# A new order of issue for the first third of a memory-attention and SwiGLU kernel

## The chip, the cores and the metric

The kernel runs on one core of a Trainium2 chip. The metric is the device time of one execution in microseconds, as the median of several runs. The core has five engines that run side by side, each with its own instruction stream: TensorE (PE, its weight loads shown apart as PEld), VectorE (DVE), ScalarE (ACT), GpSimd (POOL) and SyncE (SP), which here only starts DMA transfers.

## The reference

The inputs are q, k and v of 8 batches x 8 heads x 576 positions x 64, phi of 8 x 8 x 576 x 32, and the weights of a gated feed-forward layer, 512 wide with 1536 hidden columns.

```python
a = exp(phi - max(phi, axis=2)); a = a / (sum(a, axis=2) + 1e-9)      # softmax over the 576 positions
k_m = einsum('bhsm,bhsd->bhmd', a, k); v_m = einsum('bhsm,bhsd->bhmd', a, v)   # 32 memory slots
scores = q @ k_m^T / 8
attn = softmax(scores) @ v_m                                          # over the 32 slots
x = attn, heads side by side: 4608 x 512
xn = x / sqrt(mean(x * x) + 1e-6) * rms_g
g = xn @ w_gate; val = xn @ w_val
out = (g * sigmoid(g) * val) @ w_out
```

The three weight matrices arrive as 64-bit floating-point numbers, so they are loaded as pairs of 32-bit words and converted on the chip. q and k are large (factors of 200), and the products of the feed-forward layer are taken with every operand split into a high and a low part, three matmuls for one.

## The kernel before

All work is cut into 2785 small parts, Python functions that each issue a few instructions: one group of matmuls, one copy, one load. The program makes them in one numbered list, and `perform` calls them in the order of the list of numbers `ISSUE`. Nothing else sets the order: the scheduler of the framework is off. Each engine executes its own instructions strictly in the order in which the parts issue them, so one list sets five orders, and an instruction that has to wait holds all that stands behind it on its engine. SP is such an engine too: a load whose buffer is not free holds the loads behind it.

The parts, by stage:

- Softmax of phi (`prep`, lines 362 to 436): PE transposes a maximum (L377) and sends it back (L398), DVE subtracts it from phi (L407), ACT takes the exponential (e_bd, L416), POOL makes the sums (es, L434).
- k_m and v_m (`kv_steps`, lines 440 to 533): matmuls of k and v with e_bd (kvp, L461) and of ones with the sums (L471), scaling, transposes (kvt, L511), and copies by ACT, km (L519, part 57 for batch 0) and vt (L525). k and v of batches 0 and 1 come in large pieces (kvs, `load_half`, L334, parts 37 to 40 for batch 1), those of the others head pair by head pair (`load_kv`, L347).
- Pair 0, that is batches 0 and 1, in its own form: pieces of q (qs, L546, parts 33 to 36 and 41 to 44, two for a block of heads), a copy by ACT that orders a block (qr, L553), transposes by PE (qtp, L567) and copies of the turned q (qT, L573), scores (S, L589), their softmax on DVE and ACT (L594 to L624), x by matmuls (xp, L845), its squares summed by ACT (L856), 1/rms by a Newton iteration on DVE (L866 to L891), diagonal matrices of 1/rms by ACT (first, L803, parts 189, 190, 197), and the product of x with them by PE (ts, L811, part 191 the first, part 205 the first of the second half), whose high part ACT copies (ath, L830) and whose low part DVE makes (atl, L826).
- The later pairs (`attend_steps`): fetches of q (L645; one part is two DMA issues; parts 439 to 442 and 444 to 447 for batch 2), transposes by DVE (L654), scores (S, L670), softmax (L681 to L718).
- Weights: a load of a 128-column block of one of the three matrices (`load_w`, L927 for w_out, L930 for the others; part 810 is the third block of w_out), conversion on ACT, DVE and POOL (wex, mi, L944 to L989) into wc (gate and value) or oh and ol (w_out), a store of the converted block to DRAM (L994, L996), and later a reload (L1013, L1016) whenever a column is wanted again. wc has three buffers; raw, oh and ol two.
- The feed-forward work, in 48 column steps (12 blocks of hidden columns for each of 4 pairs): for a pair and a block of 128 hidden columns, the weights are multiplied by v_m first (vp, L1034, PE; high part xh by ACT, L1051, low part xl by DVE, L1049; parts 1118 and 1120 are the first two such copies). Then come groups of six matmuls for gate and value (pg, pv, L1069; parts 1122, 1123, 1126, 1127 and 1147 are some of the first), the gate function by ACT (L1080), the product by DVE (hf, L1085), its high part by ACT (hh, L1095) and low part by POOL (hl, L1100), and the matmuls with w_out (po, L1126), whose sum ACT or DVE adds up (acc, L1135, L1137).

PSUM, which takes the results of matmuls, is split into four banks that scores and products share and two buffers for vp.

Of the kernel before, what the change touches and what calls it, by code (L numbers as in the profile page):

```python
# [31 lines left out]
    31, 0, 37, 12, 38, 39, 13, 1, 40, 19, 14, 15, 20, 42, 2, 3, 21, 16, 17, 4, 5, 34, 22, 23, 24, 36, 18, 6,  # L32
    45, 46, 47, 25, 7, 41, 8, 9, 10, 11, 48, 43, 33, 35, 752, 745, 49, 26, 44, 60, 61, 27, 236, 52, 50, 28,
    51, 53, 55, 95, 54, 29, 223, 30, 127, 62, 57, 56, 275, 58, 63, 753, 96, 67, 64, 85, 777, 65, 755, 86, 66,
    770, 68, 32, 59, 75, 70, 238, 87, 76, 754, 72, 746, 756, 69, 757, 795, 71, 88, 77, 747, 105, 78, 97, 748,
    749, 98, 89, 79, 90, 750, 91, 237, 115, 80, 239, 106, 224, 107, 118, 81, 73, 116, 119, 128, 130, 131, 82,
    129, 751, 758, 225, 83, 92, 151, 108, 99, 117, 120, 93, 226, 84, 139, 760, 100, 94, 152, 109, 101, 110,
    102, 111, 227, 153, 112, 228, 103, 132, 778, 154, 155, 104, 113, 229, 230, 114, 74, 140, 133, 168, 121,
    134, 779, 135, 122, 231, 163, 141, 142, 169, 123, 232, 143, 164, 156, 233, 771, 136, 144, 124, 125, 165,
    137, 259, 157, 126, 145, 166, 138, 772, 167, 170, 781, 171, 172, 774, 240, 782, 146, 241, 773, 775, 234,  # L40
    158, 159, 1117, 173, 780, 147, 242, 148, 190, 235, 1118, 149, 274, 160, 1120, 197, 243, 150, 1119, 272,
    189, 191, 192, 161, 1121, 162, 174, 273, 260, 776, 175, 179, 783, 176, 796, 244, 245, 180, 798, 246, 797,
    761, 249, 247, 799, 196, 261, 194, 250, 177, 248, 198, 251, 800, 252, 178, 802, 253, 262, 254, 762, 784,
    763, 256, 764, 263, 765, 181, 182, 264, 1142, 193, 827, 766, 265, 199, 759, 183, 255, 801, 200, 266, 195,
    1123, 803, 804, 276, 805, 1122, 767, 806, 807, 1143, 201, 1145, 1144, 267, 268, 257, 820, 1146, 808, 277,
    278, 828, 202, 830, 184, 185, 186, 439, 269, 270, 271, 444, 279, 829, 1126, 831, 832, 187, 188, 785, 1127,
    1124, 440, 821, 1128, 822, 442, 204, 1125, 203, 258, 210, 280, 823, 441, 824, 281, 211, 205, 206, 208,
    212, 445, 825, 826, 833, 1185, 446, 217, 218, 768, 447, 282, 285, 286, 283, 810, 284, 209, 215, 287, 769,
    786, 1129, 289, 207, 213, 216, 288, 290, 214, 221, 222, 219, 291, 220, 787, 1132, 293, 789, 790, 788, 443,
    1130, 845, 791, 1152, 292, 448, 1131, 1136, 1133, 1138, 1134, 1137, 792, 1135, 811, 793, 449, 1139, 1186,  # L50
    1147, 1188, 812, 794, 1148, 814, 1149, 1140, 450, 1151, 815, 451, 1153, 1141, 813, 848, 1158, 1150, 816,
    462, 1154, 1157, 452, 1155, 852, 1162, 453, 1156, 846, 834, 1159, 1161, 454, 455, 847, 1167, 1160, 1210,
    849, 850, 1169, 870, 851, 1168, 465, 456, 853, 1171, 855, 463, 854, 457, 856, 458, 1172, 459, 1163, 1211,
    1173, 857, 871, 1170, 877, 858, 1174, 464, 1187, 1189, 1164, 1194, 460, 1165, 1190, 873, 1195, 461, 1192,
    1213, 872, 1204, 467, 1166, 874, 875, 876, 466, 1179, 835, 1180, 470, 1183, 1196, 1212, 1214, 878, 879,
    468, 881, 880, 1181, 882, 883, 1184, 469, 1191, 838, 836, 1193, 837, 902, 1175, 1197, 1198, 1205, 1199,
    1176, 1177, 1182, 839, 840, 471, 1178, 860, 841, 905, 295, 809, 817, 859, 472, 842, 474, 473, 1200, 475,
    1201, 1202, 476, 477, 861, 1229, 863, 903, 862, 1206, 1216, 818, 478, 294, 819, 864, 1203, 904, 1215,
    1217, 865, 866, 1207, 895, 479, 480, 481, 1225, 1219, 1218, 482, 1220, 1221, 843, 483, 896, 1230, 898,
    1222, 1223, 844, 484, 1226, 1208, 906, 488, 1227, 485, 1231, 1209, 1224, 1237, 489, 897, 899, 486, 900,  # L60
    1235, 920, 907, 487, 490, 901, 1228, 927, 1232, 309, 506, 296, 1233, 503, 507, 1239, 508, 1234, 1241, 504,
    921, 491, 908, 909, 1238, 505, 310, 492, 493, 1240, 1243, 928, 1236, 494, 923, 1245, 922, 930, 495, 924,
    925, 509, 496, 497, 885, 1253, 929, 510, 931, 498, 1251, 499, 932, 500, 910, 501, 502, 1246, 1254, 1256,
    926, 1255, 523, 1257, 1278, 524, 1252, 1321, 525, 1247, 1279, 1242, 526, 527, 945, 1280, 886, 308, 1258,
    884, 1244, 1281, 887, 1262, 1260, 889, 888, 1249, 890, 1248, 891, 892, 949, 1250, 1268, 1259, 1270, 1272,
    1261, 911, 1282, 297, 913, 1269, 298, 933, 912, 1264, 1263, 914, 1273, 1265, 1322, 915, 1297, 1271, 893,
    1274, 1266, 956, 1283, 1299, 1287, 950, 894, 1275, 1323, 1285, 1284, 951, 952, 916, 1294, 934, 1293, 947,
    511, 1267, 1286, 1324, 1325, 299, 1289, 1288, 959, 953, 1346, 1276, 512, 513, 514, 515, 516, 1389, 528,
    1290, 1291, 1298, 517, 518, 519, 520, 867, 521, 868, 522, 535, 1295, 529, 1277, 1292, 1296, 1330, 536,
    1300, 1301, 1327, 530, 1326, 1302, 1336, 1328, 954, 1311, 1338, 1329, 533, 935, 869, 1332, 534, 531, 1347,  # L70
    532, 999, 1348, 539, 1307, 1312, 540, 957, 300, 537, 538, 955, 301, 1315, 1308, 1349, 1350, 302, 1316,
    1340, 1313, 1314, 1331, 1333, 1341, 311, 1334, 303, 1337, 304, 936, 1303, 331, 958, 1339, 960, 1342, 1317,
    1304, 961, 938, 1335, 1343, 1390, 1392, 974, 1344, 1351, 1305, 1353, 312, 1306, 1391, 1393, 1365, 1345,
    313, 1414, 305, 962, 314, 977, 937, 963, 1319, 332, 306, 345, 975, 1367, 307, 344, 1352, 1309, 939, 1318,
    940, 981, 917, 1320, 346, 333, 1354, 1355, 976, 978, 1310, 1362, 1357, 1356, 979, 1361, 941, 1358, 989,
    334, 347, 1366, 335, 336, 942, 1363, 1394, 943, 1359, 1364, 1395, 1415, 1417, 1368, 337, 918, 1404, 1396,
    1369, 919, 982, 1406, 1360, 944, 980, 1371, 1377, 338, 1372, 1397, 990, 1375, 1370, 984, 1416, 992, 1418,
    991, 993, 1405, 315, 348, 316, 339, 1407, 317, 1419, 318, 320, 319, 1376, 1381, 321, 322, 323, 1409, 994,
    1421, 324, 964, 325, 995, 1382, 1398, 326, 983, 1400, 349, 328, 985, 1378, 1457, 986, 350, 1010, 987,
    1408, 541, 340, 327, 1399, 1001, 329, 967, 988, 1458, 1379, 1401, 965, 1459, 1373, 1380, 1013, 966, 341,  # L80
# [1150 lines left out]
```

## Time and profile before

| what | value |
| --- | --- |
| median of three runs | 796.77 us (792.98 to 798.15) |
| the profiled execution's own time | 792.07 us |
| its span | 790.3 us |
| mean granted clock of TensorE | 0.991 |
| PE busy | 748.9 us (95% of the span), 7496 matmuls |
| PEld busy | 639.0 us (81%) |
| DVE busy | 471.8 us (60%) |
| ACT busy | 350.9 us (44%) |
| POOL busy | 244.4 us (31%) |
| DMA | 112.86 MB, mean 143 GB/s |

The profiled execution lies 4.7 us under the median, and its span leaves 1.8 us of its time outside. The busy shares are means over the whole span. In forty equal slices of the span PE's busy share is 4, 7, 7, 7, 9, 8 and 8 tenths in the first seven, and nine tenths or more in all but two of the others; the granted clock is under nine tenths of full speed in the second slice alone. A line of the trace gives start, duration, engine, line and operation, and in brackets the idle time that the engine had before it and what ended that.

### The profile page before, as it was taken

The page shows a single profiled execution, that of the slowest core. Times are in us where ns is not written, and L with a number is a line of the kernel's source. Part 1 is how long each engine was busy: PE and PEld are TensorE (multiplying, and loading weights), DVE is VectorE, ACT ScalarE, POOL GpSimd, SP SyncE. Part 2 cuts the span into 40 slices and gives each one's busy share as a digit, 9 for nine tenths or more (in the row PEclk, how much of TensorE's full clock was granted, in tenths as well). Part 3 has the DMA queues.
Part 4 walks back from the last instruction along what each step waited for, and adds up shares of the span by engine and source line. Part 5 has one row for each costly group of instructions (what it writes and reads, how often), then busy time and mean ns, then how long its engine had stood idle before and what let it go on. Part 6 is the DMA issues. An engine that isn't in the chain of part 4 may idle for free.

```text
span 790.3 us, 18128 instructions
## 1 busy us (share of the span) xinstructions
PE 748.9 (95%) x7496; PEld 639.0 (81%) x7496; DVE 471.8 (60%) x956; ACT 350.9 (44%) x697; POOL 244.4 (31%) x209
## 2 busy tenths in 40 slices
PE   4777988999999999999999999899999999999998
PEld 2565766788887988888888888788888888888886
DVE  6698878888776676465565374655454422444443
ACT  1668767665555544532354334442432335232221
POOL 0244555354432223322433212221232212121212
PEclk9799999999999999999999999999999999999999
DMA  9947775856583652253153654222241334112113
GB/s 331 375 148 214 200 184 198 275 177 213 196 216 85 198 152 95 80 174 98 67 181 123 153 170 99 86 81 71 92 134 54 117 110 147 53 56 80 54 54 120
DMA packets 111722, 112.86 MB, mean 143 GB/s; under 512 B 61460, under 2 KB 77848, under 8 KB 111640
## 3 DMA queue, kind: packets, MB, share of 16 engines
q1 hardware_dynamic: 111640, 111.70, 45.2%
q8 instruction: 59, 0.97, 0.5%
q14 instruction: 23, 0.19, 0.1%
HBM read 89.66 MB, written 22.02 MB: 141 GB/s over the span
## 4 chain that ended last, share of the span: by engine, by line
PE 81%; DVE 6%; ACT 5%; DMA 4%; SPq 2%; issue 1%; POOL 0%; ACTq 0%; DVEq 0%
PE po L1126 36%; PE pg L1069 17%; PE pv L1069 17%; PE vp L1034 5%; PE xp L845 2%; SPq L645 2%; DMA kvs<-in_k_dram 1%; PE kvp L461 1%; DMA qs<-in_q_dram 1%; PE S L670 1%; ACT wex L944 1%; DVE phi L407 1%; ACT xh L1051 1%; DMA raw<-in_moe_w_out_dram 1%; ACT L1080 1%
## 5 line engine op out<-in xcount | busy, mean ns | idle before, releaser
L1100 POOL TENSOR_TENSOR hl<-hf,hh 128x512 fp32r<-128x512 f32 (+1 forms) x84 | 120.0, 1431 | 311.8 <-ACT hh L1095 297.9
L1085 DVE TENSOR_TENSOR hf<-pv,sg 128x256 f32<-128x256 f32 (+1 forms) x192 | 85.5, 452 | 153.1 <-PE pv L1069 110.1
L1126 PE MATMUL po<-oh,hh 128*128 128x512 f32 x432 | 172.2, 399 | 2.3 <-ACT acc L1135 1.4
L1080 ACT ACTIVATE sg<-pg 128x256 f32<-128x256 f32 (+1 forms) x192 | 77.6, 411 | 213.9 <-PE pg L1069 183.3
L1137 DVE TENSOR_TENSOR acc<-po,acc 128x512 f32<-128x512 f32 x180 | 121.0, 685 | 84.5 <-PE po L1126 84.0
L1126 PE MATMUL po<-oh,hl 128*128 128x512 f32 x432 | 170.2, 394 | 0.0
L1126 PE MATMUL po<-ol,hh 128*128 128x512 f32 x432 | 169.2, 392 | 0.0
L1095 ACT CAST hh<-hf 128x512 fp32r<-128x512 f32 (+1 forms) x96 | 64.5, 675 | 86.5 <-DVE hf L1085 86.2
L1126 PEld LDWEIGHTS po<-oh,hh 128*128 128x128 f32 x432 | 81.1, 188 | 21.8 <-ACT acc L1135 2.2
L1126 PEld LDWEIGHTS po<-oh,hl 128*128 128x128 f32 x432 | 81.2, 188 | 17.9
L1126 PEld LDWEIGHTS po<-ol,hh 128*128 128x128 f32 x432 | 81.2, 188 | 13.5
L1069 PE MATMUL pv<-ath,xh 128*128 128x320 f32 (+1 forms) x384 | 84.6, 301 | 4.3 <-ACT sg L1080 3.3
L1069 PE MATMUL pg<-ath,xh 128*128 128x256 f32 (+1 forms) x384 | 85.8, 305 | 2.4 <-DVE hf L1085 1.4
L1069 PE MATMUL pv<-ath,xl 128*128 128x320 f32 (+1 forms) x384 | 81.4, 293 | 0.0
L1069 PE MATMUL pg<-ath,xl 128*128 128x256 f32 (+1 forms) x384 | 81.3, 293 | 0.0
L1069 PE MATMUL pg<-atl,xh 128*128 128x256 f32 (+1 forms) x384 | 81.3, 293 | 0.0
L1069 PE MATMUL pv<-atl,xh 128*128 128x320 f32 (+1 forms) x384 | 81.3, 293 | 0.0
L1049 DVE TENSOR_TENSOR xl<-vp,xh 128x512 fp32r<-128x512 f32 x96 | 64.3, 682 | 28.0 <-ACT xh L1051 27.8
L1069 PEld LDWEIGHTS pg<-ath,xh 128*128 128x128 f32 x384 | 62.7, 188 | 16.7 <-issue 5.0
L1069 PEld LDWEIGHTS pv<-ath,xh 128*128 128x128 f32 x384 | 63.4, 188 | 15.3 <-ACT sg L1080 5.3
L1051 ACT CAST xh<-vp 128x512 fp32r<-128x512 f32 x96 | 54.3, 590 | 29.8 <-PE pv L1069 11.7
L1069 PEld LDWEIGHTS pv<-atl,xh 128*128 128x128 f32 x384 | 61.3, 188 | 0.0
(121 smaller groups left out, 998.0 us busy)
## 6 DMA issues: line engine op xcount, KB each, us to landing
wc<-wd SPq DMA_DIRECT2D x36, 512.0 KB, 5.5
oh<-od SPq DMA_DIRECT2D x36, 256.0 KB, 3.6
ol<-od SPq DMA_DIRECT2D x36, 256.0 KB, 3.9
out_dram<-acc SPq DMA_DIRECT2D x36, 256.0 KB, 2.2
q<-in_q_dram SPq DMA_DIRECT2D x96, 72.0 KB, 2.9
raw<-in_moe_w_val_dram SPq DMA_DIRECT2D x12, 512.0 KB, 4.7
raw<-in_moe_w_gate_dram SPq DMA_DIRECT2D x12, 512.0 KB, 4.5
raw<-in_moe_w_out_dram SPq DMA_DIRECT2D x12, 512.0 KB, 4.7
```

Source lines behind the costliest of these rows:

```text
L645: load(d["q", cc][32 * g:32 * g + 32, s], q[b, 4 * cc + 2 * s + h].rearrange("(r x) d -> r x d", r=32)[:, :, 32 * half:32 * half + 32],)
L845: nc.tensor.matmul(xp[64 * j:64 * j + 64, s, t - t0, P * cc:P * cc + P], st["at", pr][rows, t, cc, 64 * j:64 * j + 64], st["kb", 2 * pr + ...
L1034: nc.tensor.matmul(vp[32 * g:32 * g + 32, flip(b, cc), cc, :], vm[pr][rows, b, hp, 32 * (g % 2):32 * (g % 2) + 32], w[rows, hp, :], start= ...
L1049: V.tensor_tensor(out=xl[:, k], in0=src, in1=xh[:, k].bitcast(F32), op=ALU.subtract)
L1051: nc.scalar.copy(xs[i][0][:, k], src)
L1069: nc.tensor.matmul(pt[:, :N], l[:, flip(b, cc), cc, half * P:half * P + P], r[:, b, cc, t0:t0 + n, :].rearrange("p t x -> p (t x)"), start ...
L1080: nc.scalar.activation(sg[:, :N], acts[gi, b, 0][:, :N], AF.Silu)
L1085: V.tensor_tensor(out=acts[gi][:, :, b, :], in0=acts[gi, b, 1][:, :N].rearrange("p (t x) -> p t x", x=64), in1=acts[gi, b, 2][:, :N].rearr ...
L1095: nc.scalar.copy(hh, acts[gi].rearrange("p t b x -> p t (b x)"))
L1100: (V if gi and i < 12 else nc.gpsimd).tensor_tensor(out=hl, in0=acts[gi].rearrange("p t b x -> p t (b x)"), in1=hsplit[i, gi][0].bitcast(F ...
L1126: nc.tensor.matmul(po, l[:, tt, :], r, start=(m == 0), stop=(m == 5))
L1137: V.tensor_tensor(out=accs[key], in0=pt[0], in1=accs[key], op=ALU.add)
```

## The change

Only the list `ISSUE` changes. Its first 1325 numbers are put in another order, the same 1325 numbers; the last 1460 stand as they were, broken into lines elsewhere. Every part, tile, shape and buffer count stays as it is. In the trace of before the first 1325 parts fill about the first 306 us, and from the 1251st number on the two lists run side by side again but for a few parts (367, 909, 1043 to 1047, 1053) that the new list has later or earlier.

Below, the first lines of the diff and those that hold the parts named here.

```diff
--- before.py
+++ after.py
@@ -29,156 +29,159 @@
 ON_SCALAR = 21
 
 ISSUE = [
-    31, 0, 37, 12, 38, 39, 13, 1, 40, 19, 14, 15, 20, 42, 2, 3, 21, 16, 17, 4, 5, 34, 22, 23, 24, 36, 18, 6,
...
-    158, 159, 1117, 173, 780, 147, 242, 148, 190, 235, 1118, 149, 274, 160, 1120, 197, 243, 150, 1119, 272,
-    189, 191, 192, 161, 1121, 162, 174, 273, 260, 776, 175, 179, 783, 176, 796, 244, 245, 180, 798, 246, 797,
-    761, 249, 247, 799, 196, 261, 194, 250, 177, 248, 198, 251, 800, 252, 178, 802, 253, 262, 254, 762, 784,
...
-    278, 828, 202, 830, 184, 185, 186, 439, 269, 270, 271, 444, 279, 829, 1126, 831, 832, 187, 188, 785, 1127,
-    1124, 440, 821, 1128, 822, 442, 204, 1125, 203, 258, 210, 280, 823, 441, 824, 281, 211, 205, 206, 208,
-    212, 445, 825, 826, 833, 1185, 446, 217, 218, 768, 447, 282, 285, 286, 283, 810, 284, 209, 215, 287, 769,
...
-    1502, 1551, 1038, 1500, 1496, 1053, 1540, 1504, 363, 566, 1542, 1507, 365, 1552, 1505, 1511, 1039, 1040,
-    1506, 1509, 557, 1508, 1041, 1046, 558, 1517, 1044, 1042, 1553, 367, 1512, 1523, 1018, 1518, 567, 1510,
...
+    40, 31, 39, 12, 13, 14, 0, 1, 2, 3, 4, 5, 6, 19, 20, 15, 16, 17, 34, 18, 7, 21, 22, 23, 24, 45, 46, 36,
+    8, 9, 25, 26, 10, 32, 27, 28, 47, 11, 37, 48, 38, 60, 49, 61, 29, 30, 52, 51, 54, 33, 75, 62, 63, 50,
+    53, 67, 35, 85, 42, 76, 77, 64, 66, 86, 55, 56, 87, 65, 68, 70, 69, 71, 57, 752, 753, 754, 756, 43, 72,
...
+    783, 146, 147, 158, 761, 795, 798, 173, 762, 159, 160, 238, 240, 148, 241, 190, 189, 235, 242, 243, 161,
+    244, 1117, 796, 1118, 1120, 191, 197, 192, 194, 797, 162, 149, 245, 799, 150, 274, 1119, 800, 801, 179,
...
+    1144, 195, 269, 270, 1146, 829, 202, 767, 186, 187, 831, 1126, 200, 759, 1122, 1128, 832, 820, 821, 256,
+    784, 188, 822, 1147, 1124, 217, 1123, 1125, 444, 271, 279, 439, 280, 203, 204, 210, 1127, 824, 205, 281,
+    1129, 218, 823, 825, 826, 282, 206, 207, 208, 209, 221, 283, 285, 222, 286, 284, 287, 219, 220, 211,
+    833, 289, 212, 213, 214, 1132, 785, 786, 787, 215, 216, 789, 1130, 442, 1134, 441, 440, 810, 445, 443,
...
+    1597, 1555, 1017, 569, 572, 1559, 1561, 973, 1560, 1034, 1041, 1618, 570, 571, 573, 1514, 1002, 998,
+    1055, 574, 1557, 1538, 1539, 1556, 1558, 1619, 1019, 1042, 1608, 1573, 1620, 1609, 1621, 1574, 575,
+    1610, 1598, 1562, 1000, 909, 1563, 1564, 1622, 1612, 1614, 1053, 1611, 576, 1043, 1600, 577, 380, 1624,
...
```

Some of the moves: of SP's parts, the order 37, 38, 39, 40, then q pieces 42, 34, 36, 41, 43, 33, 35 becomes 40, 39, 34, 36, 37, 38, 33, 35, 42, 43, 41. Of ACT's, 190, 1118, 1120, 197, 189 becomes 190, 189, 796, 1118, 1120, 197. Of PE's, the parts between 186 and 205, which were 279, 1126 and 1127, become 1126, 1122, 1147, 1123, 279, 1127. Of SP's, 439, 444, 440, 442, 441, 445, 446, 447, 810 becomes 444, 439, 442, 441, 440, 810, 445, 446, 447, with 785 among them. The store of column 6 (part 909) goes from the 632nd place to the 1263rd, the reload of column 8 (945) from the 683rd to the 751st, that of column 13 (1001) from the 979th to the 1145th, that of column 16 (1053) from the 1163rd to the 1269th.

## Rows read from the trace of the kernel before

**Rows 1.** Windows by stage: us, each engine's busy time, granted clock, DMA share, GB/s

```profile
0.00:49.00 49.00, 30.09 (x589) 22.15 (x589) 33.66 (x107) 23.31 (x46) 11.05 (x20) 0.90 0.90 319
49.00:74.00 25.00, 18.52 (x509) 15.06 (x510) 22.43 (x59) 19.01 (x47) 12.04 (x16) 0.93 0.57 182
74.00:90.00 16.00, 13.00 (x125) 10.44 (x126) 12.88 (x41) 10.52 (x26) 8.18 (x7) 1.00 0.81 173
90.00:134.00 44.00, 38.27 (x328) 30.13 (x327) 36.83 (x61) 33.59 (x59) 20.81 (x15) 1.00 0.73 207
134.00:200.00 66.00, 65.09 (x733) 54.54 (x734) 56.45 (x111) 39.43 (x81) 31.26 (x28) 1.00 0.67 222
200.00:290.00 90.00, 89.73 (x885) 77.29 (x884) 61.83 (x119) 48.26 (x88) 29.70 (x25) 1.00 0.59 165
290.00:790.30 500.30, 494.22 (x4336) 429.42 (x4334) 247.74 (x462) 176.74 (x357) 131.31 (x102) 1.00 0.32 103
```

**Rows 2.** Three ten-microsecond windows of the start, same columns

```profile
0.00:10.00 10.00, 1.55 (x5) 0.72 (x5) 5.38 (x25) 1.28 (x1) 0.70 (x6) 1.00 0.80 272
20.00:30.00 10.00, 6.46 (x148) 4.28 (x132) 3.02 (x17) 3.97 (x8) 0.09 (x1) 0.60 1.07 378
30.00:40.00 10.00, 8.01 (x110) 6.18 (x108) 9.46 (x23) 8.80 (x20) 4.31 (x5) 0.89 1.08 373
```

**Rows 3.** Timeline of PE: start, duration, instruction, idle before it and releaser

```profile
19.53 0.89 PE L461 MATMUL kvp<-kvs,e_bd 64*32 64x128 f32 x44 [1.42 <-DMA kvs<-in_v_dram]
...
26.92 0.69 PE L511 MATMUL kvt<-ident,vb 128*128 128x128 f32 x2 [2.32 <-ACT km L519]
...
56.34 2.08 PE L811 MATMUL ts<-first 128*128 128x128 f32 x8 [2.68 <-ACT first L803]
...
73.88 0.50 PE L1069 MATMUL pg<-ath,xh 128*128 128x256 f32 x2
...
74.69 0.40 PE L1069 MATMUL pv<-ath,xh 128*128 128x256 f32 x2
...
77.66 2.05 PE L811 MATMUL ts<-first 128*128 128x128 f32 x16 [2.10 <-ACT first L803]
...
286.64 1.09 PE L1034 MATMUL vp<-wc,vm 64*32 64x256 f32 x32
...
294.77 1.96 PE L1034 MATMUL vp<-wc,vm 64*32 64x256 f32 x64
```

**Rows 4.** Chain of waits: start, length, what the end waited on

```profile
17.92 7.93 DMA qs<-in_q_dram
...
25.87 0.72 ACT qr L553
...
54.74 0.96 ACT xh L1051 x2
...
84.70 4.58 DMA raw<-in_moe_w_out_dram
```

**Rows 5.** Timeline of ACT, same columns as PE's

```profile
54.34 0.40 ACT L803 ACTIVATE first<-ident,rinv 128x128 f32<-128x128 f32 x1 [0.86 <-DVE rinv L891]
...
89.30 0.66 ACT L944 ACTIVATE wex<-raw 128x512 f32<-128x512 f32 x1 [2.54 <-DMA raw<-in_moe_w_out_dram]
```

**Rows 6.** Timeline of DVE, same columns

```profile
76.72 0.17 DVE L891 SCALAR_TENSOR_TENSOR rinv<-u,rinv 128x5 f32<-128x5 f32 x1
```

**Rows 7.** Timeline of SP's queue: start, time of the run, instructions

```profile
74.90 9.69 SPq L645 DMA_DIRECT2D q<-in_q_dram  x12
```

**Rows 8.** DMA issues of 0 to 50 us: KB each, us to landing

```profile
qs<-in_q_dram SPq DMA_DIRECT2D x8, 288.0 KB, 10.2
```

**Rows 9.** DMA issues of the whole span, same columns

```profile
raw<-in_moe_w_gate_dram SPq DMA_DIRECT2D x12, 512.0 KB, 4.5
wc<-wd SPq DMA_DIRECT2D x36, 512.0 KB, 5.5
wd<-wc SPq DMA_DIRECT2D x12, 512.0 KB, 6.0
```

282 rows, old and new, of the table ISSUE are left out of this document.

## The prediction

> **What bounds the kernel now.** I read the stages first, then TensorE's (PE's) idle times, then the chain of waits, and last the queues that feed the stages. The stages [rows 1] say where an order of issue can still gain. From 290 us on PE is busy 494.2 of 500.3 us, and the two lists are the same there. Ahead of it PE idles 18.9 us up to 49, 6.5 up to 74, 3.0 up to 90, 5.7 up to 134, then 0.9 and 0.3: 35.3 us, of which 34.1 lie ahead of 134 us. The first ten microseconds hold 8.45 of that [rows 2], spent on the first loads and the first softmax, with which both lists begin. So 25.65 us are open to the change. They are no single wait. DVE is busy 22.4 of 25 us and 36.8 of 44 us in two of these stages [rows 1], so there the second engine is nearly as full as the first; and from 20 to 40 us the DMA share is above 1 while DVE has only 3.0 us of work in the first half [rows 2]: the start waits for data, the rest for conversions and evacuations. What PE waits for is seen at its gaps [rows 3]: 1.42 us for a v piece, 2.32 us for ACT's copy of km, 2.68 us and 2.10 us for the diagonals of 1/rms ("first").
>
> The profiled execution took 792.07 us. The median is 796.77, 4.7 us above it. I work out differences against the profiled execution and add them to the median.
>
> **The change, part by part.** No part is added or taken away, so the engines' work is the same; only waits move.
>
> *The start.* SP's list has two q pieces ahead of the last two k and v pieces of batch 1, and three q pieces fewer ahead of the last piece of each of the first two q blocks. A q piece is 288 KB [rows 8], and the queue moves about 378 GB/s [rows 2], so a piece is 0.78 us: k and v of batch 1 land 1.6 us later, and the q blocks 2.3 us sooner. Before, ACT stood at a q copy until 25.87 with the copy of km queued behind it (chain of waits [rows 4]), and PE idled 2.32 us for that copy [rows 3]. In the new list ACT begins with the q blocks that land early, and the copy of km stands behind two q copies and two copies of turned q. I take the 2.32 us as gone and the 1.6 us as paid at the 1.42 us wait for v: -0.7. The bounds are -2.3 (kvs hidden) and +1.6 (the copy of km as late as before, now behind the four copies).
>
> *The first diagonals.* On ACT the list had one diagonal (part 190), two evacuations of vp (0.96 us in the chain [rows 4]), then the other diagonals; the new list has 190, 189, one conversion, then the evacuations. The first matmul of the turn by 1/rms started at 56.34 after 2.68 us [rows 3], from a first diagonal at 54.34 [rows 5]. The evacuations no longer stand between, so -1.0. DVE's chain that makes 1/rms ends the rest of that wait, and stays. Bounds 0 (the conversion, or a later ACT, takes their place) and -2.7.
>
> *The second diagonals.* In the old list only two groups of gate matmuls and a sum stand between the last matmul that makes x (part 186) and the second turn (part 205). PE runs out at the end of the second group and idles 2.10 us until 77.66 [rows 3], because 1/rms is ready at 76.9 on DVE [rows 6]. The new list puts three more groups there (1122, 1147, 1123). A group of six is 0.81 us (from 73.88 to 74.69 [rows 3]), so 2.4 us fill the 2.1: -2.1. But two of the three ran in the stage before 74 us and one near its old place ahead of 90, where they filled PE while DVE was late; there up to 2.4 us of PE time now stand open. Between 0 and +2.4 I take +2.0, near the upper end since DVE is busy 22.4 of 25 us in that stage [rows 1].
>
> *Third w_out block.* Its load (part 810) stood behind the last twelve fetches of q, which took SP 9.69 us [rows 7], 0.81 each; in the new list three parts of two fetches stand behind it instead of ahead of it, so it is issued 4.8 us sooner. It landed 4.58 us after its turn in the chain of waits [rows 4], and ACT stood 2.54 us for it at 89.30 [rows 5]. That wait goes. The last two q fetches come 0.6 us later, and DVE's transposes of them with it, and the matmuls S behind. PE got only part of ACT's 2.54 us: -1.0, bounds -2.5 and +0.6.
>
> *90 to 134 us.* PE's 5.7 us [rows 1] are many short waits behind evacuations by ACT and DVE. By the lists, of the four PSUM banks that hold scores and products, on average 3.45 are held between the 420th and the 600th part before and 2.39 after: consumers stand closer to producers, and a matmul is less often issued with no free bank. Half of the idle time: -3.0, bounds -5.7 and +2 (DVE is full in 36.8 of 44 us, and a matmul issued sooner may meet a later DVE). The Trainium skill, Perfetto Trace Analysis, section Optimization Strategy, says that the same gap repeating on the engine that should be saturated can mean too little PSUM for the next tile. By that rule the whole 5.7 us would go and the sum would be 2.7 us lower; the trace shows the waits, but not what bank each lacked. From 134 to 290 us only 1.2 us is left [rows 1]; -0.5.
>
> *Late loads.* Some seven conversions now have their load 2 to 5 us of PE's work ahead of them, against 4.5 us of landing [rows 9], and three weight columns (8, 13 and 16) are reloaded closer to their use. The tightest is column 16: its buffer is the one from which column 15 is stored, 6.0 us, and then read, 5.5 us [rows 9]: 11.5 us against 8.1 us from column 15's matmuls at 286.64 to column 16's at 294.77 [rows 3], 3.4 us short if nothing else stands between. These loads start when a buffer is free, which is mostly earlier than their place says: +1.0, bounds 0 and +10.2 (three columns late by 3.4).
>
> **Sum**: -0.7 -1.0 -2.1 +2.0 -1.0 -3.0 -0.5 +1.0 = -5.3: 786.8 against the profiled execution's 792.1, **791.5 us** against the median.
>
> **The rivals.** *The front's idle time mostly goes.* If half of the open 25.65 us goes, the time is 796.8 - 12.8 = 784. For it: the gaps that it names are removed in several places at once, and banks are held shorter. Against it: DVE is nearly full from 30 to 134 us, and its work is the same. The Trainium skill, Perfetto Trace Analysis, section Identifying the Most-Contended Engine, judges PE by the busy share of its weight loads instead of matmuls. As rows: weight loads are busy 209.6 of 290 us, and 429.4 of 500.3 after that [rows 1], 72% against 86%; at 86% the first part would take 244 us, so 46 us would be open and not 35, less the first 8.45; half of it gives 778. The mix of matmuls differs between the two parts, so I give this only 0.05 of the rival's chance of 0.28.
>
> *Nothing is gained, for DVE sets the front.* The list is executed as it stands, so it does what it says on every engine; but where DVE's work from 30 us on is the bound, a gap that is closed on PE opens at the next wait. 797, within 2 us: 0.12.
>
> *Slower: weights come late.* Place: the three reloaded columns and the seven loads. Price: 10.2 us if each column is late by 3.4, plus 0.5 of PE's time for each of seven conversions (the 3.5 us middle of the covers is 1.0 short of 4.5 landing, half of it passed on): 13.7. The start, the first diagonals and w_out still gain 2.7: 796.8 + 11 = 808. It decides from the point at which the matmuls of a column wait over 1 us for a load. For it: shorter covers; against it: PE lacks 1.2 us in all from 134 to 290 us before, so buffers are far ahead there. 0.20.
>
> **How the numbers follow.** My forecast has 0.40 and a range of its own of 786 to 797. A measurement of this kernel can tell about 1% from no change: 788.8 to 804.7. Faster than that is most of the first rival (0.25) and the lower edge of mine (0.09): 0.34. Slower is most of the slower rival, 0.16. Within it is the rest, 0.50. The range 780 to 806 leaves out the lowest of the first rival (0.08) and the upper half of the slower one (0.10).
>
> **What would show it.** Right: no 2.3 us gap of PE for km near 25 us; the turn by 1/rms under 1.7 us of wait, and at its second block none; new PE waits between 60 and 72 us; ACT not waiting for w_out near 89; PE's idle time from 90 to 134 under 3.5 us; from 290 us on the same length as before within 1 us. Wrong: idle time up to 74 us larger by over 3 us, or a wait for a weight column between 150 and 300 us.

## The result, and the profile after

The new list takes 807.21 us (median of 4 runs, 804.05 to 807.58) against 795.62 us: a ratio of 1.0137, 95% interval 1.0093 to 1.0181. It is **slower by 1.4%**, outside the range of 780 to 806 and on the other side of the forecast. The profiled execution took 804.05 us with a span of 802.3 us, 12.0 more than before.

The windows by stage of the new list, in the columns of [rows 1] (line numbers are 3 higher in the new kernel):

```profile
0.00:49.00 49.00, 28.37 (x557) 22.70 (x557) 32.80 (x102) 22.51 (x44) 9.34 (x17) 0.90 0.85 300
49.00:74.00 25.00, 17.05 (x517) 13.14 (x518) 23.58 (x62) 18.75 (x45) 13.35 (x16) 1.00 0.59 202
74.00:90.00 16.00, 12.17 (x96) 10.40 (x95) 12.67 (x42) 11.05 (x27) 7.72 (x9) 1.00 0.84 162
90.00:134.00 44.00, 36.76 (x312) 29.21 (x312) 38.06 (x53) 28.76 (x50) 17.60 (x12) 1.00 0.70 198
134.00:200.00 66.00, 61.88 (x726) 49.91 (x732) 59.54 (x105) 40.64 (x82) 34.04 (x30) 1.00 0.52 172
200.00:290.00 90.00, 88.79 (x868) 76.62 (x869) 64.35 (x122) 46.27 (x86) 31.23 (x26) 1.00 0.57 159
290.00:802.30 512.30, 505.96 (x4436) 439.74 (x4434) 255.19 (x474) 181.89 (x367) 135.47 (x105) 1.00 0.34 110
```

PE's idle time grows in every stage ahead of 290 us: 20.6 us (18.9 before), 8.0 (6.5), 3.8 (3.0), 7.2 (5.7), 4.1 (0.9), 1.2 (0.3). That is 9.7 us in all, of a span that is 12.0 longer; part of the rest is the last 1460 parts, the same in both lists, which took 1.9 us longer in this execution. TensorE's clock is not what was lost: the granted clock up to 74 us is 0.90 and 1.00 of full speed, before it was 0.90 and 0.93 [rows 1], and from there to 290 us it is 1.00 in both. **DVE's busy time** is the other thing to see. It is 486.2 us over the span and was 471.8, with the same 956 instructions. Paired part by part, with the operations' times added up, the first 1325 parts hold all of it: 260.9 us before, 276.0 now. Of these 15.1 us, 5.7 are in the clips and shifts (TENSOR_SCALAR on a weight block), 4.1 in hl, 1.7 in the third step of the conversions (wex<-raw,wex) and 1.6 in the softmax's subtraction (ex<-ex,mx).

PE's timeline of the new list, the waits that answer to [rows 3] and the new ones:

```profile
15.27 0.45 PE L401 MATMUL mr<-ident,mb 128*128 128x128 f32 x1 [2.58 <-DVE mb L396]
...
29.56 1.44 PE L592 MATMUL S<-km,qT 128*64 128x64 f32 x30 [0.49 <-ACT km L522]
...
34.43 1.12 PE L592 MATMUL S<-km,qT 128*64 128x64 f32 x16 [1.74 <-ACT qT L576]
...
51.91 1.02 PE L464 MATMUL kvp<-kv,e_bd 64*32 64x128 f32 x11 [1.53 <-ACT xp L859]
...
58.09 1.16 PE L814 MATMUL ts<-first 128*128 128x128 f32 x8 [0.48 <-ACT first L806]
...
78.93 2.05 PE L814 MATMUL ts<-first 128*128 128x128 f32 x16 [0.84 <-ACT first L806]
82.93 0.71 PE L814 MATMUL ts<-first 128*128 128x128 f32 x4 [1.95 <-ACT first L806]
...
100.59 0.51 PE L1129 MATMUL po<-oh,hl 128*128 128x512 f32 x1 [1.64 <-POOL hl L1103]
...
107.73 0.51 PE L1129 MATMUL po<-oh,hh 128*128 128x512 f32 x1 [2.10 <-DVE hf L1088]
...
121.34 1.17 PE L673 MATMUL S<-qT,km 64*32 64x288 f32 x24 [1.89 <-DVE qT L657]
...
129.48 0.50 PE L1072 MATMUL pv<-ath,xh 128*128 128x256 f32 x2 [1.16 <-DVE hf L1088]
...
148.12 0.51 PE L1129 MATMUL po<-oh,hl 128*128 128x512 f32 x1 [0.87 <-DVE hl L1103]
```

The first k matmuls now follow a transpose at 15.27 us that waited for DVE; before they ran from 12.4. The wait ahead of the first turn by 1/rms is 0.48 instead of 2.68 us, yet the turn starts 1.7 us later, since PE waited ahead of it at other places: the 2.32 us for the copy of km [rows 3] are down to 0.49, but 1.74 us for turned q and 1.53 us for the squares of x have come. The 2.10 us ahead of the second turn are now 0.84, and 1.95 ahead of its last part. From 100 us on stand waits of a length that before had not (its longest from 90 to 150 us is 0.78): for POOL's hl, DVE's hf, DVE's turned q.

What DVE and POOL did ahead of the first two of these is in their timelines. DVE of the new list:

```profile
96.27 1.70 DVE L700 TENSOR_TENSOR ex<-ex,mx 128x1152 f32<-128x1152 f32 x1
97.89 1.51 DVE L951 TENSOR_SCALAR wex<-wex 128x512 f32<-128x512 f32 x1
99.32 1.90 DVE L1103 TENSOR_TENSOR hl<-hf,hh 128x640 fp32r<-128x640 f32 x1
...
105.43 1.84 DVE L963 TENSOR_SCALAR wex<-wex 128x512 int32<-128x512 int32 x1
107.19 0.48 DVE L1088 TENSOR_TENSOR hf<-pv,sg 128x320 f32<-128x320 f32 x1
```

POOL of the new list in the same stretch:

```profile
95.46 1.29 POOL L992 TENSOR_TENSOR ol<-w,oh 128x512 fp32r<-128x512 f32 x1 [4.78 <-ACT oh L988]
96.70 2.41 POOL L984 TENSOR_TENSOR w<-mi,wex 128x512 int32<-128x512 int32 x1
99.07 1.46 POOL L1103 TENSOR_TENSOR hl<-hf,hh 128x512 fp32r<-128x512 f32 x1
...
104.86 2.13 POOL L717 TENSOR_TENSOR ex<-ex,mx 128x1152 f32<-128x1152 f32 x1 [0.69 <-DVE mx L712]
```

And the same steps on DVE in the list before (L697 is L700 of the new kernel, L948 is L951, L960 is L963, L1100 is L1103):

```profile
92.15 0.81 DVE L1100 TENSOR_TENSOR hl<-hf,hh 128x640 fp32r<-128x640 f32 x1
...
95.73 1.36 DVE L697 TENSOR_TENSOR ex<-ex,mx 128x1152 f32<-128x1152 f32 x1
97.01 0.42 DVE L948 TENSOR_SCALAR wex<-wex 128x512 f32<-128x512 f32 x1
97.35 0.48 DVE L1085 TENSOR_TENSOR hf<-pv,sg 128x320 f32<-128x320 f32 x1
97.75 0.41 DVE L960 TENSOR_SCALAR wex<-wex 128x512 int32<-128x512 int32 x1
```

The same operations are longer where POOL runs beside them: hl 1.90 us instead of 0.81, the subtraction 1.70 instead of 1.36, the clip of a weight block 1.51 instead of 0.42, its shift 1.84 instead of 0.41. The clip ends 0.29 us after POOL's w, the shift 0.28 us after POOL's subtraction, and so it is everywhere: 17 of the 72 clips and shifts of the new list took over 0.5 us, and each of them ended 0.28 or 0.29 us after an operation of POOL. They are not slowed; they wait for POOL's operation to end. POOL is held too: its w took 2.41 us, against 1.30 in the mean of before, and ended 1.14 us after DVE's subtraction; the hl that PE waits for at 100.59 stands behind it. At 107.19 hf, whose input is in PSUM, has its usual 0.48 us; it is late because the lengthened operations stand in front of it, and PE waits 2.10 us for it. Nothing of this is in the lists: POOL's block of w and DVE's conversions have no data in common there. The Trainium skill, SBUF — State Buffer, section Who interferes with whom, says that VectorE and GpSimd share one pair of SBUF ports as an exclusive lock, that a VectorE operation in one of its two-port fast modes contends for it with GpSimd, and one with two SBUF inputs with a GpSimd operation that reads SBUF, and that the order of issue decides who is blocked. The rows agree: clip, shift and hl wait where POOL began first, and POOL's w took 2.41 us where DVE's subtraction did.

The groups of DVE over the whole kernel, before and then after:

```profile
L948 DVE TENSOR_SCALAR wex<-wex 128x512 f32<-128x512 f32 x36 | 18.0, 500 | 2.9 <-ACT wex L944 2.8
L960 DVE TENSOR_SCALAR wex<-wex 128x512 int32<-128x512 int32 x36 | 17.3, 482 | 0.6
...
L1100 DVE TENSOR_TENSOR hl<-hf,hh 128x640 fp32r<-128x640 f32 x12 | 10.5, 877 | 0.9 <-ACT hh L1095 0.8
```

```profile
L963 DVE TENSOR_SCALAR wex<-wex 128x512 int32<-128x512 int32 x36 | 20.7, 576 | 0.5
L951 DVE TENSOR_SCALAR wex<-wex 128x512 f32<-128x512 f32 x36 | 20.2, 563 | 10.1 <-ACT wex L947 9.9
...
L1103 DVE TENSOR_TENSOR hl<-hf,hh 128x640 fp32r<-128x640 f32 x12 | 14.6, 1217 | 1.6 <-ACT hh L1098 1.6
```

In a count over the 72 clips and shifts of each trace:

| kernel | alone: count, mean, longest | beside POOL's two-operand operations |
| --- | --- | --- |
| before | 54, 420 ns, 430 | 18, 703 ns, 1186 |
| new list | 44, 421 ns, 444 | 28, 803 ns, 1841 |

### The profile page after: what moved, and what is told of

Read it like the earlier page. It is cut to its first block, busy times and chain, and to the rows that moved or that the text cites. A ratio compares the mean times of both kernels' runs of the same rounds, so it can differ in the third digit from the quotient of the medians.

```text
span 802.3 us, 18131 instructions
## 1 busy us (share of the span) xinstructions
PE 751.0 (94%) x7496; PEld 641.7 (80%) x7496; DVE 486.2 (61%) x956; ACT 349.9 (44%) x697; POOL 248.7 (31%) x209
## 4 chain that ended last, share of the span: by engine, by line
PE 73%; DVE 11%; ACT 5%; DMA 5%; issue 3%; SPq 2%; POOL 1%; DVEq 0%; ACTq 0%; POOLq 0%
PE po L1129 32%; PE pv L1072 16%; PE pg L1072 16%; PE vp L1037 4%; DMA kvs<-in_v_dram 2%; DMA q<-in_q_dram 2%; SPq L648 1%; PE xp L848 1%; PE kvp L464 1%; DVE wex L963 1%; DVE hf L1088 1%; DVE xl L1052 1%; DVE wex L951 1%; PE S L673 1%; DVE wex L970 1%
## 5 line engine op out<-in xcount | busy, mean ns | idle before, releaser
L1103 POOL TENSOR_TENSOR hl<-hf,hh 128x512 fp32r<-128x512 f32 (+1 forms) x84 | 120.2, 1433 | 325.0 <-ACT hh L1098 307.5
L1072 PE MATMUL pv<-ath,xh 128*128 128x256 f32 (+1 forms) x384 | 85.4, 303 | 3.8 <-ACT sg L1083 2.0
L1072 PE MATMUL pv<-ath,xl 128*128 128x256 f32 (+1 forms) x384 | 81.8, 294 | 0.2 <-DVE xl L1052 0.2
L1072 PE MATMUL pv<-atl,xh 128*128 128x256 f32 (+1 forms) x384 | 81.7, 294 | 0.0
L1072 PEld LDWEIGHTS pg<-ath,xl 128*128 128x128 f32 x384 | 61.4, 188 | 0.8 <-DVE xl L1052 0.8
```

The costliest lines, as they stand in the source:

```text
L1072: nc.tensor.matmul(pt[:, :N], l[:, flip(b, cc), cc, half * P:half * P + P], r[:, b, cc, t0:t0 + n, :].rearrange("p t x -> p (t x)"), start ...
L1103: (V if gi and i < 12 else nc.gpsimd).tensor_tensor(out=hl, in0=acts[gi].rearrange("p t b x -> p t (b x)"), in1=hsplit[i, gi][0].bitcast(F ...
```

## The experiments

Ratios are to the list of before, run beside each kernel on the same chip (medians of 794.1 to 794.7 us). The new list was not run again there. Its own ratio, 1.0137, is uncertain by 0.44%, so differences of a run to it are given as a range: from the ratios, from the medians, and from e1, which differs from it little.

| run | median us | ratio | 95% interval |
| --- | --- | --- | --- |
| e1_start_before | 807.77 | 1.0166 | 1.0137 to 1.0194 |
| e2_new_to_75 | 799.82 | 1.0063 | 1.0043 to 1.0084 |
| e3_before_to_75 | 802.62 | 1.0098 | 1.0077 to 1.0119 |
| e4_before_to_134 | 799.54 | 1.0056 | 1.0036 to 1.0075 |
| e5_new_turned | 815.64 | 1.0270 | 1.0247 to 1.0294 |
| e6_before_turned | 800.34 | 1.0079 | 1.0056 to 1.0101 |
| e7_before_pool_adds | 806.04 | 1.0151 | 1.0128 to 1.0175 |
| e8_before_pool_fills | 804.69 | 1.0133 | 1.0111 to 1.0155 |
| e9_new_fetch_first | 811.89 | 1.0219 | 1.0196 to 1.0242 |
| e10_new_fills | 799.50 | 1.0072 | 1.0046 to 1.0099 |
| e11_before_fills | 793.88 | 0.9987 | 0.9969 to 1.0006 |
| e12_start_mixed | 798.56 | 1.0052 | 1.0032 to 1.0071 |
| e13_before75_new_fills | 795.87 | 1.0011 | 0.9994 to 1.0029 |
| e14_before_wout_first | 794.08 | 1.0002 | 0.9981 to 1.0022 |
| e15_before_late_phi | 793.84 | 0.9994 | 0.9976 to 1.0012 |
| e16_before_gates_late | 794.96 | 1.0010 | 0.9991 to 1.0029 |
| e17_new_to_30 | 796.42 | 1.0023 | 1.0009 to 1.0037 |
| e18_new_to_47 | 797.61 | 1.0036 | 1.0021 to 1.0051 |

### Where in time the loss is made

```diff
 e1:  for n in ISSUE_new         # the places of parts 0 to 25, filled in the order of before
-    12 13 14 0 1 2 3 4 5 6 19 20 15 16 17 18 7 21 ...
+    0 12 13 1 19 14 15 20 2 3 21 16 17 4 5 22 23 24 18 6 ...
 e2, e17, e18:
+    ISSUE = new[:330] + [n for n in before if n not in new[:330]]    # 110 and 190 in e17, e18
 e3, e4:
+    ISSUE = before[:330] + [n for n in new if n not in before[:330]]   # 600 in e4
```

> The new list, but the 26 parts of the first phi softmax (batches 0 and 1) stand in the order of the list before, in the places that the new list has for such parts. Theory (the start: in the new list DVE takes the halves of phi in an order that starts the first k and v matmuls at 15.6 us instead of 12.4): those matmuls start at 12.4 to 13 us again, and the time falls by 2 to 3.2 us, to 804 to 805. Rival (the 3 us are hidden behind the loads of k, v and q that follow): the matmuls start earlier, and the time stays at 806 to 808.

It misses. The first k matmuls start at 12.6 us, 3 us ahead of the new list. The second turn by 1/rms starts at 77.13 us, 1.8 ahead of the new list and 0.5 ahead of before; its last part, at 81.13, is 0.5 behind before. (The lead of 1.9 us at 82 us of which the expectation of e12 speaks is thus one over the new list, not over before.) At 309 us the same instructions are 9.6 us late, against 10.1 in the new list. A lead of 3 us at the start is worth nothing to the loss behind it.

> The first 330 parts of the new list (about 75 us), then all others in the order of the list before. Theory (half of the loss is made in the first 75 us, by the start and by waits for diagonals and evacuations): about 5 us slower than before, 800 to 801. Rival (weights reloaded late, or DVE held up after 90 us, make all of it): no different from before, 795 to 797.

> The first 330 parts of the list before (about 75 us), then all others in the order of the new list. Theory (half of the loss is made after 75 us, where DVE is 90% busy and its operations are stretched when POOL's run beside them): about 5 us slower than before, 800 to 801, with DVE busy 8 to 12 us more than before. Rival (all of the loss is the late start, handed on): 795 to 797. Rival (late weights make all of it): 806 to 808.

> The first 600 parts of the list before (about 134 us), then all others in the order of the new list. Theory (what is lost from 134 to 200 us is DVE's lateness, partly inherited from the stages before): 2 to 4 us slower than before, 798 to 800. Rival (late reloads of weight columns 8, 13 and 16, all behind this point, make the loss): over 6 us slower, 802 or more, with PE waiting for weights.

The loss splits: 0.63% come from the first 75 us and 0.98% from what is behind them, of which 0.56% is left where the new list starts at 134 us only. The two parts add up to the 1.4 to 1.7% of the whole. (e3's 802.6 us lie between what theory and rivals had named.) In e3 DVE's first 1325 parts take 12.4 us more than before, in e4 4.2, in e2 2.8. In none of these traces does a matmul of a gate or value column wait for a load; the new list has one wait of 0.34 us for a reloaded block of w_out.

> The first 110 parts of the new list (loads, phi, first copies of q and km, about 30 us), then all others in the order of before. Theory (the later k and v of batch 1 and the copy of km behind the q copies, 1.8 us at km, make the loss): 2 to 5 us slower than before, 796 to 799. Rival (this start is hidden, as the phi order was): 793 to 795.

> The first 190 parts of the new list (about 47 us, with the scores and the softmax of pair 0), then all others in the order of before. Theory (all of the 5 us lie ahead of the 190th part; part of it in the softmax of pair 0, where PE waits 1.5 us at 50 us for POOL's normalisation): 798 to 801. Rival (it lies in the turn by 1/rms and the first gates, behind the 190th): 793 to 796.

The medians of the first 75 us rise step by step: 0.23% to 30 us, 0.36% to 47, 0.63% to 75. The intervals of neighbouring steps overlap, and e18 came between the values that theory and rival had named, so the split is rough. PE's timeline of e18:

```profile
34.16 0.70 PE L589 MATMUL S<-km,qT 128*64 128x64 f32 x16 [1.74 <-ACT qT L573]
36.06 1.51 PE L567 MATMUL qtp<-ident,qr 128*128 128x128 f32 x8 [1.20 <-ACT qr L553]
```

Scores and transposes wait for q blocks whose copies the new list has later (1.74 and 1.20 us). These waits are not what makes e17's 2 us: it has the first of them too, and from 39 to 66 us its matmuls run within 0.3 us of before (medians of the same instructions). It falls 1.9 us behind at 72 us, where its list is that of before, since ACT waits for a weight block that in the trace of before had landed when its turn came at 67.47:

```profile
69.63 0.68 ACT L944 ACTIVATE wex<-raw 128x512 f32<-128x512 f32 x1 [2.14 <-DMA raw<-in_moe_w_val_dram]
```

This is one execution; whether the block is late in the others is not shown. In the new list the copy of km is at 28.31 us on ACT, at 26.50 before, behind the copies that the list puts in front of it.

> The list of before, with only the 26 parts of the first phi softmax in the order of the new list. Theory (this late start makes most of what the new list loses in the first 75 us): the first k matmuls start at 15 to 16 us, and the time rises by 2 to 5 us, to 796 to 799. Rival (the start is hidden behind the loads, and the 5 us come from the waits for diagonals and from x): 793 to 795.

> The first 330 parts of the new list with the first phi softmax in the order of before (as in the first experiment), then all others in the order of before. In the first experiment this start was 1.9 us ahead of before at 82 us. Theory (a lead at 82 us is kept where the order behind it is that of before): 1 to 2 us faster than before, 792.5 to 793.5. Rival (the lead is lost at the seam, as the second experiment lost time there): 795 to 799.

```diff
 e15:  for n in ISSUE_before     # the places of parts 0 to 25, filled in the order of the new list
 e12:  ISSUE = e1_list[:330] + [n for n in before if n not in e1_list[:330]]
```

The late phi order alone costs nothing (k matmuls at 15.5 us, same time), and mending it in the first 75 us of the new list wins 0.1%, within the intervals. So the 5 us of the first 75 us are not the phi order; which moves make them was not cut further.

### Do the longer DVE operations make the rest?

```diff
 e5, e6 (new list, list of before), in convert:
+    def turned(x):
+        return x.rearrange("p (a b) -> p b a", a=32)
-    V.tensor_scalar(out=ex.bitcast(F32), in0=ex.bitcast(F32), scalar1=EXP_LO, ...)
+    V.tensor_scalar(out=turned(ex.bitcast(F32)), in0=turned(ex.bitcast(F32)), scalar1=EXP_LO, ...)
     (and the shift in the same way)
```

> The new list; the two in-place operations by which DVE clips and shifts a block of weights (128x512, 0.42 us alone, up to 1.5 us beside a POOL operation) walk through the block in strides of 16 elements instead of one. Theory (DVE's stretched operations make the loss after 75 us, and a strided walk is not stretched by POOL): none of the 72 operations is over 0.8 us, DVE is busy less in the first 200 us than with the new list, and the time falls by 2 to 5 us, to 802 to 805. Rival (the stretch falls in DVE's slack, and the order of PE's work makes the loss): the operations change, the time stays at 806 to 809. Rival (a strided walk is stretched as well, or is itself slower than the stretch): operations at 0.6 us and more, time 808 or over.

> The list of before with the same strided walk. Theory: here these operations were seldom stretched, so a strided walk costs as much as it is slower alone: 795 to 798, and the difference of the two lists falls from 12 us to 4 to 9. Rival (the stretch is harmless): no change in either, a difference of 11 to 13 us.

The premise failed, as the third rival had it: a strided clip or shift takes 0.62 us alone and is stretched all the same, to 968 ns in the mean of 31 in e5. What the pair tells is the price of DVE time: DVE's first parts take 15.8 us more in e5 than in the new list and the kernel 8 to 11 us more; 18.3 us more in e6 than before cost 5.7. Half of DVE's added time or more shows in the new list, a third before.

```diff
 e7, behind the first step of each of the 36 conversions, list of before:
+    for _ in range(4): nc.gpsimd.tensor_tensor(out=pad, in0=ident[:, :112], in1=ident[:, :112], op=ALU.add)
 e8, in the same place:
+    for _ in range(8): nc.gpsimd.memset(pad, 0.0)
```

> The list of before; behind each of the 36 first steps of a conversion POOL has four more additions (128x112, about 0.45 us each) whose result nobody reads. Theory (additions on POOL stretch DVE's operations, and DVE's time in the first 200 us is PE's time): DVE busy 6 to 15 us more in the first third, 3 to 8 us slower, 798 to 803. Rival (POOL's time is off the path, and DVE's stretch with it): DVE busy more, but 794 to 797.

> As the run before, but POOL's extra work is eight fills (128x112) of the same buffer, which read nothing. Theory (only POOL's additions, which read two operands, stretch DVE): POOL is busy longer as in the run with additions, DVE's time stays within 2 us of before, 794 to 797. Rival (any POOL work does it, by its own lateness): the same loss as with the additions.

Both lose alike, and more than was expected of the additions, so this pair does not separate the theories: POOL's extra operations take 65.9 and 61.9 us, PE waits up to 3.1 and 2.8 us for POOL's sums of the softmax (es, 0.6 before), DVE's first parts take 12.2 and 8.0 us more, and PE's granted clock fell to 0.79 from 74 to 90 us in both. Beside short operations alone the clips and shifts are hardly longer (469 ns with additions, 435 with fills).

```diff
 e10, e11 (new list, list of before), in convert:
-    nc.gpsimd.tensor_tensor(out=w, in0=m, in1=ex, op=ALU.add)
+    nc.gpsimd.tensor_tensor(out=w[4 columns], in0=m[4 columns], in1=ex[4 columns], op=ALU.add)
+    for _ in range(2): nc.gpsimd.memset(w, 0.0)
     (the subtraction that makes ol in the same way; the weights, and so the output, are zero)
 e13:  the same, with ISSUE = before[:330] + [n for n in new if n not in before[:330]]
```

> The new list; in the conversion of weights POOL's two operations of 128x512 elements (1.3 us alone) add or subtract on only 4 columns and then fill the whole block with zeros twice (about 1.3 us), so POOL is as long busy, but reads nothing meanwhile; weights and output are zero. Theory (POOL's two-operand operations stretch DVE's, and DVE's late operations make at least half of the loss after 75 us; fills do not stretch: 435 ns against 420 in the run with extra fills): DVE's time in the first third falls by 6 to 10 us against the new list, and the time by 3 to 6 us, to 801 to 804. Rival (the stretch lies in DVE's slack): DVE's time falls, the time stays at 806 to 809.

> The list of before with the same fills. Theory: here fewer operations coincide, so DVE's time falls by 3 to 5 us and the time by 0 to 2, 793 to 795; the difference of the two lists falls from 12 to 7 to 10 us. Rival: 794 to 796, and a difference of 11 to 13 us.

> The list of before for the first 330 parts (about 75 us), the new list behind it, and POOL's operations in the conversions replaced by fills as in the tenth run (weights and output zero). Theory (the first 75 us and the coinciding operations are the whole loss): as fast as the list of before with fills, 792 to 796. Rival (a third cause behind 75 us, as late reloads or a late q): 798 or more.

This decides it. With fills the new list takes 799.5 us, below the theory's 801 to 804 and 5 to 8 less than without, while the list of before, with the same zeros, stays where it was. What is left of the difference, 5.6 us, is the size of the first 75 us alone (e2). And with the order of before up to 75 us and fills (e13) the loss is gone: 1.0011, its interval holds 1; without fills the same list (e3) lost 0.98%. DVE's hl, the windows of two stages, and PE's first two late waits of the new list, in e10:

```profile
L1112 DVE TENSOR_TENSOR hl<-hf,hh 128x640 fp32r<-128x640 f32 x12 | 9.9, 821 | 1.6 <-ACT hh L1107 1.6
```

```profile
90.00:134.00 44.00, 38.48 (x344) 30.85 (x346) 38.05 (x56) 30.68 (x54) 20.41 (x32) 1.00 0.70 198
134.00:200.00 66.00, 64.92 (x782) 54.77 (x775) 58.23 (x119) 40.26 (x82) 32.33 (x54) 1.00 0.58 189
```

DVE's operations ahead of these two, and POOL's beside them:

```profile
97.60 0.42 DVE L951 TENSOR_SCALAR wex<-wex 128x512 f32<-128x512 f32 x1
97.94 0.81 DVE L1112 TENSOR_TENSOR hl<-hf,hh 128x640 fp32r<-128x640 f32 x1
...
103.78 1.85 DVE L963 TENSOR_SCALAR wex<-wex 128x512 int32<-128x512 int32 x1
```

```profile
96.66 1.09 POOL L988 TENSOR_TENSOR w<-mi,wex 128x4 int32<-128x4 int32 x1
97.80 1.27 POOL L990 MEMSET w<- 128x512 f32 x2
```

```profile
100.53 0.50 PE L1138 MATMUL po<-oh,hl 128*128 128x512 f32 x1 [1.53 <-POOL hl L1112]
...
106.08 0.50 PE L1138 MATMUL po<-oh,hh 128*128 128x512 f32 x1 [0.51 <-DVE hf L1097]
```

DVE's hl is 821 ns in the mean instead of 1217; PE idles 1.1 us from 134 to 200 instead of 4.1; its wait for hf is 0.51 instead of 2.10. The shift ahead of that hf is as long as in the new list, 1.85 us, for POOL's softmax subtraction beside it is no conversion. What changed is the work in front: the clip took 0.42 instead of 1.51 us and hl 0.81 instead of 1.90, and the shift begins 1.65 us earlier. A fill is 0.53 us, so it blocks a clip for a shorter time, not at all less surely: clips and shifts beside fills alone took 589 ns in the mean of 7. DVE's hl at 97.94, with two inputs in SBUF, kept its time beside a fill.

POOL's lateness stayed. Its w of four columns was held to 1.09 us, the fills behind it ended at 99.07 (w at 99.11 in the new list), and PE's wait for POOL's hl is still 1.53 us. Over the first 1325 parts POOL's operations took 4.7 us more in the new list than in the list of before, and 4.0 more with fills in both. DVE's took 15.1 us more, and 4.8 with fills. The same holds behind 75 us. POOL's excess is 3.1 us in e3 (over before) and 3.5 in e13 (over e11); DVE's falls from 12.4 to 3.4, and the loss goes. So the runs put most of it on DVE's late results; POOL's longer operations, which stayed, leave at most the 0.3% to which e13's interval reaches.

### Single terms of the prediction

```diff
 e9 (new list):       -  810, 445 ... 446, 447          +  445, 446, 447, 810
 e14 (list of before): -  445 ... 446 ... 447 ... 810    +  810, 445 ... 446 ... 447
 e16 (list of before): -  1123 ... 1122 ... 186    +  186, 1122, 1123
```

> The new list, but the three q fetches 445, 446, 447 stand ahead of the third w_out load (810) again, as before. Theory (the load put ahead of the fetches delays the turned q and all that hangs on it between 82 and 106 us, where the new list falls 4 us behind): DVE's second transpose of q is 1 to 3 us earlier, and the time falls by 2 to 4 us, to 803 to 805. Rival (that stage is lost to DVE and POOL stretching each other, and the fetch is early enough in either order): 806 to 809.

> The list of before with one part moved: the third w_out load (810) ahead of the q fetches 445, 446, 447. Theory (the prediction's term: ACT's 2.5 us wait for that block goes, PE gets 1 us; the ninth run lost 4.7 us by the opposite move in the new list): 1 to 3 us faster, 791 to 793. Rival (the fetches are late in its place): 794 to 797.

e9 goes the other way, 4 to 7 us slower than the new list: the load ahead of the fetches is not the fault there. ACT waits for the block in e9, and PE for ACT:

```profile
92.79 0.66 ACT L944 ACTIVATE wex<-raw 128x512 f32<-128x512 f32 x1 [4.21 <-DMA raw<-in_moe_w_out_dram]
```

```profile
93.83 0.50 PE L1069 MATMUL pg<-ath,xh 128*128 128x256 f32 x2 [3.11 <-ACT sg L1080]
```

In the list of before the same move is worth nothing. ACT's 2.54 us wait [rows 5] is gone in e14, and DVE waits 1.81 us for the q that now comes later (0.81 before):

```profile
86.13 0.68 ACT L944 ACTIVATE wex<-raw 128x512 f32<-128x512 f32 x1
```

```profile
87.07 1.38 DVE L654 STREAM_TRANSPOSE qT<-q 128x1152 f32<-128x1152 f32 x1 [1.81 <-DMA q<-in_q_dram]
```

> The list of before with two groups of gate matmuls (1122, 1123) moved behind the last matmul that makes x (186), where the new list has them. Theory (the prediction's second diagonals: they fill the 2.1 us wait ahead of the second turn and leave 1.6 us open where they stood): the wait at 76 us falls under 0.8 us, waits grow between 65 and 72 us, and the time stays within 1 us, 793 to 795. Rival (where they stood DVE held PE anyway, and the wait is won): 792 to 793. Rival (the sums and gates behind them come late and hold DVE): 796 or more.

As the theory had it: the 2.10 us wait [rows 3] is gone, and PE waits 1.61 and 2.98 us where the gates stood (it waited 0.49 and 0.90 us there before). The granted clock of this execution was at its lower level from 74.3 us on for 6.8 us, so the groups that were moved took longer than at their old place:

```profile
68.75 0.54 PE L461 MATMUL kvp<-kv,e_bd 64*32 64x128 f32 x9 [1.61 <-ACT e_bd L416]
...
74.77 1.13 PE L845 MATMUL xp<-vb,at 64*64 64x128 f32 x16 [2.98 <-ACT at L757]
```

No version tried is faster than the list of before by more than its interval.

## Why the prediction was wrong, point by point

**The step that failed** is the one ahead of the sum: "No part is added or taken away, so the engines' work is the same; only waits move." The instructions are the same, their durations are not. DVE's first 1325 parts took 15.1 us more, because more of them ran beside POOL's two-operand operations (28 clips and shifts instead of 18), and DVE had little room: from 90 to 134 us it was busy 36.8 of 44 us, against PE's 38.3 [rows 1]. e10, e11 and e13 put 5 to 8 of the 12 us on that. The rest, some 5 us, is made in the first 75 us, where the terms come to -1.8 us (-0.7 -1.0 -2.1 +2.0) and PE's idle time up to 74 us grew by 3.2: the waits that the prediction looked at shrank, and the new ones at other places had no term. The prediction read DVE's load from the stages, and took every duration as fixed; a row that would have warned stood in the trace of before, where clips of the same shape took 0.42 us and 1.19.

*The start*, forecast -0.7 between -2.3 and +1.6. The wait for km did go, as forecast (2.32 to 0.49 us), though the copy came 1.8 us later; in its place PE waits 1.74 us for turned q, which had no term. e17 took 2 us more in the median (0.7 to 2.9), but its trace is within 0.3 us of before from 39 to 66 us, so how the start costs 2 us is open. The prediction took the first ten microseconds as the same in both lists; the order of the phi softmax there delays the first k matmuls by 3.2 us, and it happens to be hidden (e15).

*First diagonals*, -1.0: the wait shrank from 2.68 to 0.48 us, but the turn starts 1.7 us later. *Second diagonals*, -2.1 and +2.0: e16 shows both halves as described, and their sum of nothing.

*Third w_out block*, -1.0: 0.0 in the list of before (e14); the wait passed to DVE's transpose of q, at the upper bound's side. In the new list the move is worth 4 to 7 us (e9): the price of a move depends on the order around it.

*90 to 134 us*, -3.0: PE's idle time rose from 5.7 to 7.2 us. Banks held for a shorter time won nothing, since PE now waited for what DVE and POOL delivered late (2.10, 1.89, 1.64 and 1.16 us). *134 to 290 us*, -0.5: it rose from 1.2 to 5.3 us, the largest miss of the stages. *Late loads*, +1.0: PE waited once for a reloaded block, for 0.34 us, so the term was near 0.

*The rivals.* The slower one gave 808 us, which is what came, but by late weights, and what it named as its point of decision did not happen: the number was right by coincidence. "DVE sets the front" was nearest in mechanism, with DVE's work still taken as the same. The 778 us worked out from the weight loads did not come either; whether the time that they called open can be won, no run here shows. Of the prediction's own signs of being wrong the first came: PE's idle time up to 74 us grew by 3.2 us, over the 3 that it had named.

**Open** stays which moves cost the 5 us of the front.

## What to carry to other kernels

A new order of issue can change how long operations take, not only when they start. Before forecasting a reordering, look in the trace for one shape with two durations, see what ran beside the long ones, and ask how often the new order will bring these two together. A wait that a move removes on one engine is worth what the next engine does with it: two of the moves here removed the wait that they were aimed at and changed the time by nothing.

## What the hardware showed that was not expected

A two-operand operation of POOL and a clip, shift, hl or softmax subtraction of DVE on SBUF excluded each other until the one that ran had ended: 0.42 us became up to 1.84, and POOL's 1.30 became 2.41. DVE operations with an input in PSUM kept their time (hf of 320 columns in the new list: 487 ns in the mean of 29 beside POOL's operations, 486 in the mean of 67 without). A strided walk over the block did not lift it (622 ns alone, 968 beside POOL).

PE's granted clock fell for some microseconds between 70 and 90 us in several of the profiled executions, after short idle times. In e4 it was 0.74 of full speed in the mean from 70 to 80 us (1.00 before), so for part of that time PE ran at 1.2 instead of 2.4 GHz; ahead of and in that stretch PE had idled 0.49, 0.96, 0.55 and 1.25 us. The order did not cause this: up to 134 us e4's list is that of before, and its same matmuls are 0.7 us late at 90 us. Nor is the clock e4's loss: the mean granted clock of its nine runs is 0.986, that of the 14 runs of before beside them 0.987.
